# Scores of two head pairs in one visit: six half-filled PSUM banks become six nearly full ones

## The chip, the cores and the metric

The kernel runs on one core of one Trainium2 chip. The metric is the time of one execution on the device in microseconds (us), the median of several runs. One execution is also taken by the hardware profiler; its span, from the first to the last instruction, is a little shorter than the time of that same execution, and all stage times below are counted from the span's start.

## The reference

```python
def _attn_ref(q, k, v):                     # q, k, v: (8, 8, 576, 64) float32
    scores = scale * np.matmul(q, k.transpose(0, 1, 3, 2))
    rel = pos[:, None] - pos[None, :]
    mask_local = (rel >= 0) & (rel < 32)
    mask_strided = (rel >= 0) & (pos[None, :] % 32 == pos[:, None] % 32)
    # heads 0..3 take mask_local, heads 4..7 mask_strided; then softmax
    return np.matmul(attn, v)
def _moe_ref(x, w_in, w_out, alpha):        # x: (4608, 512), d_ff 2048
    h = x @ w_in
    g = np.maximum(h, 0.0) + alpha * np.minimum(h, 0.0)
    return g @ w_out
```

Attention with a different sparse mask on each half of the heads feeds a two-layer network with a PReLU between the layers. The attention output of all heads of a token is one row of x.

## The kernel before

**Attention.** The 8 batches have 8 heads each, and the kernel works on pairs of heads, 32 in all: pair g belongs to batch g//4, pairs with g%4 of 0 and 1 are local, those with 2 and 3 strided. Two neighbouring pairs of one kind are a unit u = g//2. The masks leave small dense blocks: a local head has 6 blocks of 96 queries, a strided head 8 blocks of 72. For a block, TensorE multiplies 128 keys (72 used for a strided head) by the queries over 64 rows, the head dimension. The two heads of a pair lie on partitions 0 to 63 and 64 to 127, so that their products, each half the height of the array, alternate between the halves. `score_both` (L427) makes the scores of one pair: the first group of blocks goes into `sp`, a tile of two PSUM banks, one for each head, the second into two banks `sph` of the pool `ps`. ScalarE takes exponentials into an SBUF tile `et` (L464 for `sp`, L474 twice for `sph`), and GpSimd multiplies by the 0/1 mask (L468, L470, L477). The two exponentials on `sph` are put on a list `defer`, from which each later step of attention takes one (L660); in the second half of a chunk the first of them is done at once. `pv_piece` (L486), here written P(g,a), multiplies the weights of group a of pair g by V into a `ps` bank `pv`, and VectorE evicts it with a reciprocal (L521) and a multiply (L523). Strided pairs have three such groups and local pairs two. The result is transposed into `xT`, on TensorE (`x_piece`) or by DMA (`x_dma`, with `x_copy` on ScalarE for a strided pair).

**The network.** Tokens are worked in 9 chunks of 512, n = 0 to 8. From n = 1 a chunk is a loop of 30 slots (L1025). Slots 0 to 15 (L1 here) each make one tile of the first layer: four products of 512 columns into a bank `hb` (L678), a Relu of the negative on ScalarE into `neg` (L697), and on VectorE the PReLU into `gT` (L700, deferred by the list `late` until the end of the next step). Slots 16 to 29 (L2 here) are the second layer in seven products of quarters, two slots each, with eight products of 256 columns in a slot (L811). Its operands `gsum` are sums of quarters of `gT`, made mostly on VectorE (L760), in part on GpSimd at slots 5, 9 and 13. It accumulates in three banks named A, B and C; C is used by the sixth product only (slots 26 and 27; in n = 1 slots 18 and 19).

**Order.** All work is issued in the order in which the program writes it, on each engine (`keep`). Attention from batch 2 on is cut into 97 pieces (L577 to L645), and after each slot a pace `acc` (L1039) decides how many pieces to issue. For pair g the pieces are S (the scores of pair g), P(g-1,0), perhaps a transpose of queries, X(g-2), P(g-1,1), perhaps a transpose of keys, and P(g-1,2). Some pieces carry extra work: `cast_v` on GpSimd in the first two pieces that are not S, `x_dma`, `load_d`, `load_v` or `transpose_d` after the last P, `transpose_l` or `x_copy` after the first piece. DMAs are issued from GpSimd (all that convert float32 to float16) and from SyncE.

**PSUM.** There are eight banks: `sp` has two, the pool `ps` three in rotation, and three are `hb0` to `hb2`, which `hbank` gives out to the first layer in turn and which A, B and C name in the second.

Of the kernel before, what the change touches and what calls it, by code (L numbers as in the profile page):

```python
# [9 lines left out]
F32 = mybir.dt.float32  # L10
F16 = mybir.dt.float16
ALU = mybir.AluOpType
AF = mybir.ActivationFunctionType
# [19 lines left out]
def kernel(  # L33
# [42 lines left out]
    mfirst, mother, mstr = mmul[:, 0:288], mmul[:, 96:192], mmul[0:72, 288:360]  # L76
# [22 lines left out]
    kTs = [cpool.tile([128, 2, (768, 672)[i]], F16, name=f"kT{i}") for i in range(2)]  # L99
    vls = [cpool.tile([128, 24, 65], F16, name=f"vl{i}") for i in range(2)]  # L100
    vss = [cpool.tile([128, 4, 8, 65], F16, name=f"vs{i}") for i in range(2)]
    ets = [cpool.tile([128, 800], F16, name=f"et{i}") for i in range(NE)]
    x16s = cpool.tile([80, 1024], F16)
    qks = {nm: cpool.tile([80, 4, 512], F16, name=f"{nm}sd") for nm in "qk"}

# [4 lines left out]
    def load_qk(b, strided, nm):  # L110

        h0 = 4 if strided else 0
        src = q if nm == "q" else k
        if strided and b:
            t16 = hpool.tile([128, 2, 512], F16, tag=f"{nm}s", bufs=2, name=f"{nm}s")
            cast16[(b, True, nm)] = t16
        else:
            t16 = hpool.tile([128, 2, 512], F32, tag=f"{nm}l", bufs=2, name=f"{nm}l")  # L120
            loaded[(b, strided, nm)] = t16
        base = src[b, h0 : h0 + 1, 0:1, :]
        eng = nc.sync if (b > 2 and not strided) or (b == 0 and strided) else nc.gpsimd
        if b == 0 and strided and nm == "q":
            eng = nc.scalar
        keep(eng.dma_start(t16, bass.AP(
            tensor=base.tensor, offset=base.offset,
            ap=[[8 * D, 64], [2 * S * D, 2], [S * D, 2], [1, 8 * D]])))
# [30 lines left out]
            keep(nc.sync.dma_start_transpose(o, qks[nm].rearrange("p h c -> p (h c)")))  # L159

    def cast_s(b, nm, eng):
        t16 = hpool.tile([128, 2, 512], F16, tag=f"{nm}s", bufs=2, name=f"{nm}s")
# [73 lines left out]
    ectr = {"i": 0}  # L236
# [3 lines left out]
    def make_pair(g):  # L240
        P = Pair()
        P.g, P.b, P.hp = g, g // 4, g % 4
        P.strided = P.hp >= 2
        P.pr = P.hp % 2
        P.n, P.w = (8, 72) if P.strided else (6, 96)
        u = g // 2
        P.dx = P.b >= DX and P.strided
        P.lx = P.b >= LX and not P.strided
        P.xd = P.b >= DX and P.hp < (2 if P.b == DX else 3)
        if P.dx or P.lx:  # L250
            P.qT, P.kT = (z[u % 2].rearrange("r e c -> r (e c)") for z in (qTs, kTs))
# [4 lines left out]
        if P.lx:  # L256
            P.sgroups = ([0, 1, 2, 3], [4, 5])
        P.et = {}
        P.x16 = None
        return P  # L260
# [162 lines left out]
    defer, defer_et = [], {}  # L423
    late = []
    second = {"on": False}

    def score_both(P):  # L427

        w, r = P.w, 72 if P.strided else 128
        for i in range(2):  # L430
            et = ets[ectr["i"] % NE]
            ectr["i"] += 1
            if i:
                sps = [pspool.tile([128, 512], F32, tag="ps", name="sph") for _ in range(2)]
            else:
                sp = pbpool.tile([128, 2, 512], F32, tag="sp", name="sp")
                sps = [sp[:, y] for y in range(2)]
            grp = P.sgroups[i]
            n = w * len(grp)
            for x, t in enumerate(grp):  # L440
                if P.dx:
                    q0 = k0 = 80 * (4 * (2 * P.pr + t % 2) + t // 2)
                elif P.lx:
                    j = 3 * (2 * P.pr + t % 2) + t // 2
                    q0, k0 = 96 * j, 128 * j
                else:
                    q0, k0 = w * t, 32 + 72 * t if P.strided else 96 * t
                for y in range(2):
                    hf = slice(64 * y, 64 * y + 64)
                    keep(nc.tensor.matmul(  # L450
                        sps[y][:, w * x : w * x + w], P.kT[hf, k0 : k0 + 128],
                        P.qT[hf, q0 : q0 + w], start=(x == 0), stop=(x == len(grp) - 1),
                        skip_group_check=True))
                    P.et[(2 * (t // 2) + y, t % 2) if P.dx or P.lx else (t, y)] = (et, n * y + w * x)
            ev = et[0:r, 0 : 2 * n]
            if not P.strided and i == 0 and not P.lx:
                mv = ev.rearrange("r (y c) -> r y c", y=2)
                m = mfirst.unsqueeze(1).to_broadcast([r, 2, n])
            else:
                z = 2 * w if P.lx and i == 0 else 0  # L460
                mv = ev[:, z:].rearrange("r (c f) -> r c f", f=w)
                m = (mstr if P.strided else mother).unsqueeze(1).to_broadcast([r, (2 * n - z) // w, w])
            if i == 0:
                keep(nc.scalar.activation(  # L464
                    ev.rearrange("r (y c) -> r y c", y=2), sp[0:r, :, 0:n], AF.Exp, scale=SCALE))
                if P.lx:
                    fv = ev[:, 0 : 2 * w].rearrange("r (c f) -> r c f", f=w)
                    keep(nc.gpsimd.tensor_tensor(  # L468
                        fv, fv, mfirst[:, 0:96].unsqueeze(1).to_broadcast([r, 2, w]), op=ALU.mult))
                keep(nc.gpsimd.tensor_tensor(mv, mv, m, op=ALU.mult))  # L470
                continue

            def ex(y):
                keep(nc.scalar.activation(  # L474
                    ev[:, n * y : n * y + n], sps[y][0:r, 0:n], AF.Exp, scale=SCALE))
                if y:
                    keep(nc.gpsimd.tensor_tensor(mv, mv, m, op=ALU.mult))  # L477

            defer_et["et"] = et
            if second["on"]:  # L480
                ex(0)
                defer.append(lambda: ex(1))
            else:
                defer.extend([lambda: ex(0), lambda: ex(1)])

    def pv_piece(P, a):  # L486
        run_masks(P)
        while defer and any(P.et[z][0] is defer_et["et"] for z in P.et):
            defer.pop(0)()
        if P.x16 is None:  # L490
            if P.xd and P.strided:
                P.x16 = x16s
# [25 lines left out]
        w = P.w  # L518
# [52 lines left out]
    def Pv(g, i):  # L571
        return lambda: pv_piece(pairs[g], i)
# [4 lines left out]
    for g in range(7, npair + 2):  # L577
# [75 lines left out]
    def attn_step(end):  # L653
        run_masks()
        if pos["i"] < end:
            pieces[pos["i"]][1]()
            pos["i"] += 1
        while late:
            late.pop(0)()
        if defer:  # L660
            defer.pop(0)()


    gTs = {}
# [94 lines left out]
        }[which]  # L759
        keep(eng.tensor_tensor(o[:, k0:k1], x[:, k0:k1], y[:, k0:k1], op=op))  # L760

    lay, held = {}, {}

    def store(n, i, j, osb, mts=(0, 1)):

# [310 lines left out]
```

## Time and profile before

| | us |
|---|---|
| median of 3 runs | 299.58 (299.42 to 299.84) |
| the profiled execution | 300.0 |
| its span | 298.1 |
| chunk n=1, L1 and L2 | about 59 to 75, 75 to 91.7 |
| chunk n=3, L1 and L2 | about 122.8 to 138.1, 138.1 to 153.0 |
| score visits of the pairs 8 to 31 (L450) | 24, from 61.6 to 226.9 |

The page gives, for each engine, how long it was busy and in which of 40 slices. A line of the timeline gives start, length, engine, line, operation, tiles (out<-in), shape and count of like instructions merged into one row; a bracket at its end is the time in which the engine idled before it and what it waited for. Rows of TensorE overlap, since matmuls are pipelined: a product's row is longer than the time in which the next can start.

### The profile page before, as it was taken

Reading aid. Unit: us, or ns where it says so; the run is one execution under the profiler, and the core shown is the slowest. Engines: PE = TensorE matmul, PEld = TensorE weight load, DVE = VectorE, ACT = ScalarE, POOL = GpSimd, SP = SyncE. Lnnn points to the kernel's source line nnn. Section 1 sums busy time; section 2 is a strip of 40 time slices with the busy share of each in tenths; the row PEclk is TensorE's granted clock in tenths of the full one; section 3 lists DMA queues with packets and bytes.
Section 4 is the critical chain, followed back from the end, with each engine's and each line's share of the span. In section 5 each row is a group of like instructions: output and inputs, shape, how many; then the busy total and the mean of one; then the engine's idle time right before and its main releaser. Section 6 shows DMA issues by size and latency. Waiting matters only on the chain.

```text
span 298.1 us, 7107 instructions
## 1 busy us (share of the span) xinstructions
PE 289.9 (97%) x2808; PEld 193.6 (65%) x2808; DVE 227.8 (76%) x427; ACT 173.5 (58%) x325; POOL 168.5 (57%) x182
## 2 busy tenths in 40 slices
PE   7899998999999999999999999999999999999995
PEld 3664445644886478646898887468746864784584
DVE  5788868979975988488848894889488858946872
ACT  3566556888557773776377636763676257406620
POOL 8952289359757996777777778665555003101300
PEclk9999999999999999999999999999999999999999
DMA  7999999995998969999999999993811140022004
GB/s 219 204 202 207 205 238 266 170 175 178 177 154 186 111 100 127 173 192 160 132 209 177 138 141 182 184 144 54 201 22 21 24 141 0 2 71 73 0 2 141
DMA packets 102273, 41.01 MB, mean 138 GB/s; under 512 B 80720, under 2 KB 99424, under 8 KB 102240
## 3 DMA queue, kind: packets, MB, share of 16 engines
q0 software_dynamic: 56336, 19.25, 61.1%
q1 hardware_dynamic: 45632, 20.78, 35.3%
q10 hardware_dynamic: 272, 0.52, 0.6%
q8 instruction: 22, 0.36, 0.6%
q14 instruction: 11, 0.09, 0.1%
HBM read 38.60 MB, written 9.44 MB: 161 GB/s over the span
## 4 chain that ended last, share of the span: by engine, by line
PE 80%; DMA 11%; POOL 4%; issue 2%; DVE 2%; ACT 1%; POOLq 0%
PE hb L678 36%; PE hb L811 32%; DMA ks<-in_k_dram 6%; PE pv L512 4%; DMA win<-in_moe_w_in_dram 3%; PE sp L450 2%; DMA ql<-in_q_dram 2%; PE hb L715 2%; PE opl L811 1%; PE xp L533 1%; PE tp L280 1%; DVE gT L700 1%; PE sph L450 1%; POOL ql L217 1%; POOL vl L205 0%
## 5 line engine op out<-in xcount | busy, mean ns | idle before, releaser
L678 PE MATMUL hb<-xT,win 128*128 128x512 f16 (+1 forms) x616 | 127.2, 357 | 0.0
L700 DVE SCALAR_TENSOR_TENSOR gT<-neg,oma,hb 128x512 f16<-128x512 f32 x138 | 100.7, 744 | 33.0 <-ACT neg L697 26.3
L697 ACT ACTIVATE neg<-hb 128x512 f32<-128x512 f32 x138 | 82.1, 597 | 32.7 <-PE hb L678 31.5
L678 PEld LDWEIGHTS <-win 128*128 128x128 f16 x640 | 60.0, 98 | 53.8
L760 POOL TENSOR_TENSOR gsum<-gT 128x512 f16<-128x512 f16 x23 | 26.5, 1152 | 68.9 <-DVE gT L700 68.9
L811 PEld LDWEIGHTS <-gsum 128*128 128x128 f16 x512 | 47.3, 98 | 6.0 <-DVE gsum L760 0.5
L811 PEld LDWEIGHTS <-gT 128*128 128x128 f16 x384 | 35.9, 98 | 6.0 <-issue 0.5
L470 POOL TENSOR_TENSOR et<-et,mmul 128x576 f16<-128x576 f16 (+1 forms) x24 | 30.6, 1274 | 14.6 <-issue 7.8
L823 ACT COPY o<-hb 128x512 f32<-128x512 f32 (+1 forms) x32 | 18.1, 569 | 32.5 <-PE hb L811 32.5
L523 DVE TENSOR_TENSOR x<-pv,rc 96x384 f16<-96x384 f32 (+2 forms) x65 | 34.5, 531 | 2.2
L811 PE MATMUL hb<-wout,gT 128*128 128x256 f16 x248 | 30.8, 273 | 0.1
L811 PE MATMUL hb<-wout,gsum 128*128 128x256 f16 x248 | 30.5, 272 | 0.0
L811 PE MATMUL hb<-wsum,gsum 128*128 128x256 f16 x248 | 30.3, 273 | 0.0
L477 POOL TENSOR_TENSOR et<-et,mmul 72x576 f16<-72x576 f16 (+2 forms) x24 | 29.3, 1220 | 0.4 <-ACT et L474 0.4
L826 DVE TENSOR_TENSOR o<-hb,o 128x512 f32<-128x512 f32 (+1 forms) x24 | 16.3, 681 | 17.0 <-PE hb L811 12.5
L464 ACT ACTIVATE et<-sp 72x576 f16<-72x576 f32 (+2 forms) x24 | 16.4, 685 | 20.6 <-PE sph L450 17.2
L512 PEld LDWEIGHTS <-et 72*128 72x128 f16 (+1 forms) x416 | 21.9, 98 | 8.0 <-issue 1.3
L474 ACT ACTIVATE et<-sph 72x288 f16<-72x288 f32 (+2 forms) x48 | 17.8, 388 | 0.0
L521 DVE RECIPROCAL rc<-pv 72x6 f32<-72x6 f32 (+2 forms) x80 | 14.5, 181 | 2.9 <-PE pv L512 2.4
L715 PE MATMUL hb<-wout,gT 128*128 128x512 f16 x64 | 15.6, 379 | 0.2 <-ACT osb L720 0.2
L811 PE MATMUL hb<-wsum,gT 128*128 128x256 f16 x120 | 15.3, 273 | 0.0
L760 DVE TENSOR_TENSOR gsum<-gT 128x512 f16<-128x512 f16 (+2 forms) x17 | 14.7, 865 | 0.2
(117 smaller groups left out, 318.0 us busy)
## 6 DMA issues: line engine op xcount, KB each, us to landing
out_dram<-o SPq DMA_DIRECT2D x31, 256.0 KB, 3.1
stv<-in_v_dram POOLq DMA_DIRECT2D x8, 288.0 KB, 8.4
vl<-in_v_dram POOLq DMA_DIRECT2D x6, 384.0 KB, 9.3
wout<-in_moe_w_out_dram POOLq DMA_DIRECT2D x4, 512.0 KB, 16.9
qsd<-in_q_dram POOLq DMA_DIRECT2D x6, 288.0 KB, 7.6
ksd<-in_k_dram POOLq DMA_DIRECT2D x6, 288.0 KB, 7.1
kl<-in_k_dram SPq DMA_DIRECT2D x3, 512.0 KB, 5.1
ql<-in_q_dram POOLq DMA_DIRECT2D x3, 512.0 KB, 6.4
```

Source lines behind the costliest of these rows:

```text
L470: keep(nc.gpsimd.tensor_tensor(mv, mv, m, op=ALU.mult))
L474: keep(nc.scalar.activation(ev[:, n * y : n * y + n], sps[y][0:r, 0:n], AF.Exp, scale=SCALE))
L477: keep(nc.gpsimd.tensor_tensor(mv, mv, m, op=ALU.mult))
L512: keep(nc.tensor.matmul(pv[:, 65 * x : 65 * x + 65], et[0:r, c : c + 128], v16[0:r, 2 * P.pr + hh, t, :] if P.strided else v16[:, 6 * (2 * ...
L523: keep(nc.vector.tensor_tensor(P.x16[0:w, c0 : c0 + 64 * nb].rearrange("r (c e) -> r c e", e=64), pvv[:, :, 0:64], rc[0:w, 0:nb].unsqueeze ...
L678: keep(nc.tensor.matmul(hps[:, dst : dst + w], win16[:, kk, 128 * m : 128 * m + 128], xT[:, kk, src : src + w], start=(first and kk == kks ...
L697: keep(nc.scalar.activation(neg, hps, AF.Relu, scale=-1.0))
L700: keep(nc.vector.scalar_tensor_tensor(gTs[n][:, m, :], neg, oma[:, m : m + 1], hps, op0=ALU.mult, op1=ALU.add))
L715: keep(nc.tensor.matmul(ops, gTs[n][:, kf, 128 * mt : 128 * mt + 128], wout16[:, kf, :], start=(kf == 0), stop=(kf == 15)))
L760: keep(eng.tensor_tensor(o[:, k0:k1], x[:, k0:k1], y[:, k0:k1], op=op))
L811: keep(nc.tensor.matmul(dst, lhs[:, kf, 128 * mt : 128 * mt + 128], rhs[:, kf, :], start=(first and own and kf == 0), stop=(kf == 7), skip ...
L823: keep(nc.scalar.copy(o, x))
```

## The change

`score_both` is replaced by `score_unit`, which makes the scores of both pairs of a unit, A and Bp, in one piece. It takes `sp`, three banks of `ps` (c3, c1, c2) and a sixth bank c4: one from `hbank` in L1, bank C in L2. With nb = 5 blocks of a local head or 7 of a strided one, `sp` takes the first nb blocks of both heads of A, c1 and c2 those of the two heads of Bp, and c3 and c4 the last block of both pairs. A bank is filled to 480 columns (local) or 504 (strided), c3 and c4 to 192 or 144. The matmuls are the same, in the order `sp`, c3/c4, c1/c2, always alternating between the halves. There are five exponentials for a unit instead of six, in new wide tiles `evs` (e1, e2) and an `et` tile (e3); those on c3 (in L1 only), c1 and c2 go to `defer`. The masks of a unit are five multiplies on GpSimd.

In the order of pieces, S comes for even g only, after P(g-1,0) instead of before it, and an empty piece N follows it; cast_v counts N as a place. For odd g the list begins with P(g-1,0). The tiles `evs` also serve as the buffers of the strided queries and keys of batches 0 and 1, and the six memsets of the `et` tails on GpSimd (160 columns) become four of 64.

```diff
@@ tiles @@
-    ets = [cpool.tile([128, 800], F16, name=f"et{i}") for i in range(NE)]
+    ets = [cpool.tile([128, 640], F16, name=f"et{i}") for i in range(NE)]
+    evs = [[cpool.tile([128, 1088], F16, name=f"ev{i}{j}") for j in range(2)] for i in range(2)]
@@ scores @@
-    def score_both(P):
...
+    def score_unit(u):
+
+        A, Bp = pairs[2 * u], pairs[2 * u + 1]
+        w, r, nb = A.w, 72 if A.strided else 128, 7 if A.strided else 5
+        n = nb * w
+        (e1, e2), e3 = evs[u % 2], ets[u % 2]
+        sp = pbpool.tile([128, 2, 512], F32, tag="sp", name="sp")
+        c3, c1, c2 = [pspool.tile([128, 512], F32, tag="ps", name="sph") for _ in range(3)]
+        c4 = lay["Cf"] if second["on"] else hbank()
+        rest = [(A, nb), (Bp, nb)]
+        streams = [
+            [(A, s, sp[:, 0], w * s) for s in range(nb)]
+            + [(P, s, c3, w * z) for z, (P, s) in enumerate(rest)]
+            + [(Bp, s, c1, w * s) for s in range(nb)],
+            [(A, s, sp[:, 1], w * s) for s in range(nb)]
+            + [(P, s, c4, w * z) for z, (P, s) in enumerate(rest)]
+            + [(Bp, s, c2, w * s) for s in range(nb)],
+        ]
+        for x in range(2 * nb + 2):
+            for y in range(2):
+                P, s, o, c = streams[y][x]
...
+        def ex3():
+            ev = e3[0:r, 0 : 4 * w]
+            ex(ev[:, 0 : 2 * w], c3[0:r, 0 : 2 * w])
+            mask(ev.rearrange("r (c f) -> r c f", f=w),
+                 (mstr if A.strided else mother).unsqueeze(1).to_broadcast([r, 4, w]))
+
+        def ex2():
+            ex(e2[0:r, n : 2 * n], c2[0:r, 0:n])
+            masks(e2)
+
+        ex(e1[0:r, 0 : 2 * n].rearrange("r (y c) -> r y c", y=2), sp[0:r, :, 0:n])
+        ex(e3[0:r, 2 * w : 4 * w], c4[0:r, 0 : 2 * w])
+        masks(e1)
+        if second["on"]:
+            ex3()
+        else:
+            defer.append(((e3,), ex3))
+        defer.append(((e2,), lambda: ex(e2[0:r, 0:n], c1[0:r, 0:n])))
+        defer.append(((e2,), ex2))
@@ order of pieces @@
-        if okA:
-            seq.append(("S", lambda a=a: score_both(pairs[a])))
         if okP:
             seq.append(("P", Pv(p, 0)))
+        if okA and a % 2 == 0:
+            seq.append(("S", lambda a=a: score_unit(a // 2)))
+            seq.append(("N", lambda: None))
@@ start @@
         if m == 6:
-            for t in ets:
-                keep(nc.gpsimd.memset(t[:, 640:800], 0.0))
+            for t in evs[0] + evs[1]:
+                keep(nc.gpsimd.memset(t[:, 1024:1088], 0.0))
```

More of the change, by code (lines that the diff above doesn't have):

```diff
@@ L116, in load_qk @@
         if strided and b:
-            t16 = hpool.tile([128, 2, 512], F16, tag=f"{nm}s", bufs=2, name=f"{nm}s")
+            t16 = evs[b]["qk".index(nm)][:, 0:1024].rearrange("p (f c) -> p f c", f=2)
             cast16[(b, True, nm)] = t16
@@ L161, in cast_s @@
     def cast_s(b, nm, eng):
-        t16 = hpool.tile([128, 2, 512], F16, tag=f"{nm}s", bufs=2, name=f"{nm}s")
+        t16 = evs[b]["qk".index(nm)][:, 0:1024].rearrange("p (f c) -> p f c", f=2)
         if eng[0] == eng[1]:
@@ L255, in make_pair @@
         P.pgroups = ([0, 1, 2], [3, 4, 5], [6, 7]) if P.strided else P.sgroups
-        if P.lx:
-            P.sgroups = ([0, 1, 2, 3], [4, 5])
         P.et = {}
@@ L421, in score_piece @@
         keep(nc.gpsimd.tensor_tensor(ev, ev, m, op=ALU.mult))
-    defer, defer_et = [], {}
+    defer = []
     late = []
+    lay = {}
     second = {"on": False}
-    def score_both(P):
[L429 to L440, printed above, removed]
+    def score_unit(u):
[18 more added lines that the diff above has]
+                P, s, o, c = streams[y][x]
@@ L441, in score_both @@
                 if P.dx:
-                    q0 = k0 = 80 * (4 * (2 * P.pr + t % 2) + t // 2)
+                    q0 = k0 = 80 * (4 * (2 * P.pr + s % 2) + s // 2)
                 elif P.lx:
-                    j = 3 * (2 * P.pr + t % 2) + t // 2
+                    j = 3 * (2 * P.pr + s % 2) + s // 2
                     q0, k0 = 96 * j, 128 * j
                 else:
[L447 to L458, printed above, removed]
-            else:
[L460 to L484, printed above, removed]
+                    q0, k0 = w * s, 96 * s
@@ new lines, in score_unit, with mask @@
+                hf = slice(64 * y, 64 * y + 64)
+                keep(nc.tensor.matmul(
+                    o[:, c : c + w], P.kT[hf, k0 : k0 + 128], P.qT[hf, q0 : q0 + w],
+                    start=(c == 0), stop=(c == (1 if s == nb else nb - 1) * w), skip_group_check=True))
+                key = (2 * (s // 2) + y, s % 2) if P.dx or P.lx else (s, y)
+                P.et[key] = (e3, 2 * w * y + c) if s == nb else (e1 if P is A else e2, n * y + c)
+        def mask(v, m):
+            keep(nc.gpsimd.tensor_tensor(v, v, m, op=ALU.mult))
@@ new lines, in masks @@
+        def masks(e):
+            ev = e[0:r, 0 : 2 * n]
+            if A.lx:
+                fv = ev[:, 0 : 2 * w].rearrange("r (c f) -> r c f", f=w)
+                mask(fv, mfirst[:, 0:96].unsqueeze(1).to_broadcast([r, 2, w]))
+                fv = ev[:, 2 * w :].rearrange("r (c f) -> r c f", f=w)
+                mask(fv, mother.unsqueeze(1).to_broadcast([r, 2 * nb - 2, w]))
+                return
+            k = 4 if A.strided else 3
+            fv = ev.rearrange("r (y c) -> r y c", y=2)
+            if A.strided:
+                m = mstr
+                for lo, hi in ((0, k), (k, nb)):
+                    mask(fv[:, :, w * lo : w * hi].rearrange("r y (c f) -> r y c f", f=w),
+                         m.unsqueeze(1).unsqueeze(1).to_broadcast([r, 2, hi - lo, w]))
+            else:
+                mask(fv[:, :, 0 : w * k], mfirst.unsqueeze(1).to_broadcast([r, 2, w * k]))
+                mask(fv[:, :, w * k :].rearrange("r y (c f) -> r y c f", f=w),
+                     mother.unsqueeze(1).unsqueeze(1).to_broadcast([r, 2, nb - k, w]))
@@ new lines, in ex @@
+        def ex(o, i):
+            keep(nc.scalar.activation(o, i, AF.Exp, scale=SCALE))
+        def ex3():
[7 more added lines that the diff above has]
+        ex(e1[0:r, 0 : 2 * n].rearrange("r (y c) -> r y c", y=2), sp[0:r, :, 0:n])
@@ L486, in pv_piece @@
+        ex(e3[0:r, 2 * w : 4 * w], c4[0:r, 0 : 2 * w])
[6 more added lines that the diff above has]
+        defer.append(((e2,), ex2))
     def pv_piece(P, a):
         run_masks(P)
-        while defer and any(P.et[z][0] is defer_et["et"] for z in P.et):
-            defer.pop(0)()
+        used = [P.et[t, y][0] for t in P.pgroups[a] for y in range(2)]
@@ L490, in pv_piece @@
+        while any(e is z for es, _ in defer for e in es for z in used):
+            defer.pop(0)[1]()
         if P.x16 is None:
@@ L660, in attn_step @@
         if defer:
-            defer.pop(0)()
+            defer.pop(0)[1]()
     gTs = {}
@@ L760, in g_sum @@
         keep(eng.tensor_tensor(o[:, k0:k1], x[:, k0:k1], y[:, k0:k1], op=op))
-    lay, held = {}, {}
+    held = {}
     def store(n, i, j, osb, mts=(0, 1)):
```

## The prediction, made before the result was known

> **What bounds the kernel now.** I read the page first (busy time, slices, chain), then the waits, then the timelines of single engines around score visits.
>
> ```profile
> PE 289.9 (97%) x2808; PEld 193.6 (65%) x2808; DVE 227.8 (76%) x427; ACT 173.5 (58%) x325; POOL 168.5 (57%) x182
> ...
> PEclk9999999999999999999999999999999999999999
> ```
>
> TensorE is the bound, at full clock, and the chain is 80% PE. The waits view (us in total, times, longest) adds a line:
>
> ```profile
> PEld L450 <- issue: 6.8, 22, 0.4
> ```
>
> So the weight loads of the score matmuls (L450) sat idle 22 times, about 0.31 us each: something happens whenever PE turns to half-height products. The timeline of PE in chunk n=3 (start, length, last column the count) shows what:
>
> ```profile
> 142.57 0.60 PE L811 MATMUL hb<-wsum,gsum 128*128 128x256 f16 x4
> 143.10 0.34 PE L450 MATMUL sp<-qT,kT 64*128 64x96 f16 x8
> 143.28 0.25 PE L450 MATMUL sph<-qT,kT 64*128 64x96 f16 x4
> 143.47 1.05 PE L811 MATMUL hb<-wsum,gsum 128*128 128x256 f16 x8
> 144.59 0.34 PE L512 MATMUL pv<-vs,et 72*128 72x65 f16 x6
> ```
>
> Eight L811 products take 0.875 us, 109 ns each. Four from 142.57 end at 143.01, but L450 starts at 143.10: 0.09 lost going in. Eight score products take 0.18 (a pair of heads per 45 ns, side by side), so the twelve end near 143.37; L811 resumes at 143.47, 0.10 lost going out. A third loss: L811 should end at 144.35, but the next pv starts at 144.59, 0.24 late. Its PSUM bank is the reason, as VectorE's timeline shows:
>
> ```profile
> 142.21 0.55 DVE L523 TENSOR_TENSOR x16s<-pv,rc 72x384 f16<-72x384 f32 x1
> 142.69 1.21 DVE L760 TENSOR_TENSOR gsum<-gT,gsum 128x2048 f16<-128x2048 f16 x1
> 143.82 0.17 DVE L521 RECIPROCAL rc<-pv 72x4 f32<-72x4 f32 x1
> 144.03 0.42 DVE L523 TENSOR_TENSOR x16s<-pv,rc 72x256 f16<-72x256 f32 x1
> 144.37 1.21 DVE L760 TENSOR_TENSOR gsum<-gT 128x2048 f16<-128x2048 f16 x1
> 145.50 0.18 DVE L521 RECIPROCAL rc<-pv 72x6 f32<-72x6 f32 x1
> 145.72 0.56 DVE L523 TENSOR_TENSOR x<-pv,rc 72x384 f16<-72x384 f32 x1
> ```
>
> VectorE runs without a gap from 138.98 to 146.28. The eviction ending at 144.45 frees the ps bank that the pv at 144.59 takes (0.14 later). GpSimd's timeline in n=1:
>
> ```profile
> 62.95 1.28 POOL L470 TENSOR_TENSOR et<-et,mmul 128x576 f16<-128x576 f16 x1 [7.85 <-issue]
> 64.18 2.01 POOL L217 COPY vs<-stv 72x1024 f16<-72x1024 f16 x2
> ...
> 82.49 0.76 POOL L197 DMA_DIRECT2D stv<-in_v_dram  x1
> 85.59 1.27 POOL L470 TENSOR_TENSOR et<-et,mmul 128x576 f16<-128x576 f16 x1 [2.35 <-ACT et L464]
> 86.83 1.26 POOL L477 TENSOR_TENSOR et<-et,mmul 128x576 f16<-128x576 f16 x1
> 91.58 2.02 POOL L217 COPY vs<-stv 72x1024 f16<-72x1024 f16 x2 [3.49 <-DMA stv<-in_v_dram]
> ```
>
> Here the cast of batch 3's V waits for its load until 91.58, with the score masks safely ahead of it.
>
> [...]
>
> **The change, part by part** (L1 = slots 0 to 15, L2 = slots 16 to 29 of a chunk; a slot of L2 is 0.875 us, a tile of L1 0.864 us, a pv piece 0.19).
>
> 1. *Visits.* 24 become 12, with the same 336 matmuls. A visit costs 0.46 us (143.01 to 143.47), of which 12 or 16 matmuls stream for 0.26; what goes is one entry and one exit, 0.09+0.10 plus 0.01 on the first product after: 0.208. 12 x 0.208 = **-2.5**.
>
> 2. *The pv wait* above recurs in n=3, 4, 5 (at 144.6, 174.9, 205.1), 0.24 each. With two ps tiles fewer between, that pv finds its bank free: **-0.7**.
>
> 3. *GpSimd memsets* (L986): six of 128x160, 1.12 us on the chain at 40.8, become four of 128x64: 0.30 by columns, 0.75 by count. PE waits 0.7 for GpSimd soon after. I take **-0.4**, ends 0 and -0.8.
>
> 4. *Third ps bank in L2.* The visit now wants all three ps banks, and the piece in front of it is P(g-1,0), whose pv holds one; before, S came first and took two older banks. n=3: L2's slot 4 ends at 143.01, the pv adds 0.19, slot 5 0.875, so the visit starts at 144.16, and c2 (eighth of twelve pairs, 7 x 0.043 later) is wanted at 144.47. VectorE evicts that pv at 145.50 to 146.28 because its queue, in program order, is full. The pv of P(4n+5,1) also moves three slots later in L1, so that VectorE enters L2 0.14 later. 146.28+0.14+0.14 = 146.56: PE waits 2.09 us with all of lin2 behind it. n=4 and 5 repeat the pattern 30 us apart (evictions end 176.58, 206.74): 3 x 2.07 = **+6.2**. n=2: eviction could end 115.90, plus 0.28, wanted 115.41: **+0.7**. n=1: **+0.2**. c4 is lin2's bank C there, unused until slot 26: nothing.
>
> 5. *c4 in L1* takes one of lin1's three banks, so the reuse distance falls. Relu 0.60 and PReLU 0.745 with their latencies free a tile's bank 1.63 us after its last product (0.20+0.60+0.03+0.745+0.05); three tiles give 1.73. The tile after the visit takes the bank of the tile before last: free at 1.63-0.86 = 0.77, wanted at 0.72, plus VectorE's arrears from the P before (0.14 after two tiles, 0.31 after one): 0.05 in the first visit, 0.2 in four, 0.35 in two: 1.55. ScalarE's three exponentials in a row (estimate 0.92+0.2+0.2, from 576 wide in 0.54 start to start and 0.9 ns a column) hold the next Relu by about 0.1, nearly inside the slack. **+1.6**, ends 0.5 and 2.6. Exponential columns are the same; only bunching costs.
>
> 6. *GpSimd in n=1.* First visit at 61.5: two masks of it from 63.3, the e3 mask to 66.3, V casts 2.0 to 68.3, gsum 1.1 to 69.4, and only then e2's first mask, to 70.6. P(9,0) moves ahead of S, two slots earlier: 61.5+0.77+8 tiles+2 pieces = 69.5. **+1.1**, ends 0 and 1.5. Second: cast_v(3,0) now goes ahead of unit 6's masks and waits for DMA till 91.58 (GpSimd reaches that load at about 82.5 as before). Cast 0.98, first mask 1.27: 93.85. P(12,0), at 90.39 before, comes at about 91.5. **+2.3**; ends 0 (load lands early) and 4.8 (loads of vl, qsd, ksd leave some 3 us later and crowd it).
>
> 7. *Moved and hidden.* load_d of c+1 goes three slots later: 133.2 becomes about 136.3, landed by 144.7 (median 7.6), and SP's transposes ran at 145.78 behind x_dma anyway; without that cover SP is late, PE is not, since the data is used a chunk later. x_copy moves from S's slot to P(g,0)'s: ScalarE is idle there now that the exponentials come earlier. load_v and load_l keep their slots. Elsewhere the first cast_v (1.0) precedes e1's masks, five slots before their use. One more mask per unit costs GpSimd about 0.2, hidden likewise.
>
> Sum: -2.5-0.7-0.4+6.2+0.7+0.2+1.6+1.1+2.3 = **+8.5** on the profiled execution's 300.0 us (span 298.1 and 1.9 around it), that is 308.5. The median of the runs is 299.6, 0.4 lower: **308.1**.
>
> **Rivals.** (A) All waits as above: 308.1, 305.5 to 311 by the ends; 0.58. (B) PSUM waits only: n=1's masks come in time, -3.4: 304.7, down to 301.5 with VectorE's arrears one piece smaller (3 x 0.7) and L1 at its low end; for it, GpSimd idles 2.35 and 1.58 in n=1; against it, strict order at the cast; 0.22. (C) The other side: banks are free when wanted. Place: c2 in L2, and c4's neighbours. It decides at 144.4: if the preceding pv is evicted by then (VectorE ahead of its gsum steps by 1.9 us), 8.7 goes: 299.4, and 296.0 if the pv also relieves n=1. For it: that pv is issued 1.5 us earlier than before. Against: VectorE has no gap to take it in. 0.13. (D) Heavier: late masks also hold P(2u,0) elsewhere, or V lands late: 312 to 314; 0.07. That the change doesn't merge visits I exclude[...].
>
> **Numbers.** 0.2% (0.6 us) is about what a measurement can tell. C splits into faster 0.08 and same 0.05; the rest, 0.87, is slower. Leaving out C and D (0.2) gives 301.5 to 311.
>
> **What would show it.** Right: 12 visits of about 0.73 us plus a hole before c2 of some 2 us in n=3, 4, 5, ended by the eviction of the preceding pv; no 0.24 hole at the next pv; a PE wait on masks at P(12,0) near 91 to 94. Wrong: c2 following c1 without a hole, or the V cast of n=1 landing before 89.

## The result, and the profile after

The changed kernel takes **325.21 us** (median of four runs, 324.29 to 326.36) against 299.71 us (299.42 to 300.34) for the kernel before on the same chip: a ratio of **1.085** (95% interval 1.081 to 1.089). The forecast was 308.1, with a range up to 311. The direction and most of the places were right; the size was not. The span of the profiled execution grew from 298.1 to 324.6 us, by 26.5.

The first thing to look at in the page of the changed kernel is TensorE's busy share beside the clock row:

```profile
PE 299.8 (92%) x2808; PEld 199.0 (61%) x2808; DVE 233.9 (72%) x427; ACT 172.7 (53%) x313; POOL 172.2 (53%) x186
...
PEclk9999999999996999999799987999799999999999
```

TensorE does the same 2808 products, but it is busy 9.9 us longer, and it idles 24.8 us of the span instead of 8.2. The clock row, which was all nines, has dips in the slices near 100, 155 to 165, 195 to 200 and 230 us. The forecast noted the full clock of before and had no term for a change in it. The waits view (us in total, times, longest) says who was waited for:

```profile
PEld L456 <- DVE x L546: 6.5, 5, 2.0
...
PE sph L456 <- DVE x L546: 5.8, 4, 1.9
...
PE pv L535 <- POOL ev L463: 5.1, 3, 4.2
...
PEld L835 <- DVE gsum L784: 3.5, 7, 1.1
...
PEld L456 <- issue: 3.4, 11, 0.4
```

The last row answers to the 22 idle weight loads of before (6.8 us): half of them are gone, as forecast. The others are new. In TensorE's timeline of chunk n=3 the first pair of them shows as the hole that was forecast in front of c2, with another in front of c1, which was not:

```profile
155.11 0.39 PE L456 MATMUL sp<-qT,kT 64*128 64x96 f16 x10
...
156.31 0.21 PE L456 MATMUL sph<-qT,kT 64*128 64x96 f16 x1 [0.73 <-DVE x16s L546]
158.43 0.58 PE L456 MATMUL sph<-qT,kT 64*128 64x96 f16 x9 [1.91 <-DVE x L546]
158.94 4.01 PE L835 MATMUL hb<-wout,gsum 128*128 128x256 f16 x24
```

By the starts of single products, c1 comes 0.89 us late and c2 another 2.08. Then look at the last row: 24 products of 256 columns end 4.01 us after their start; at the 109 ns of before they need 24 x 0.109 = 2.6 us and the tail of the last. Eleven of the single starts stand 213 ns apart: the clock is halved there, in the records from 158.05 to 161.47. VectorE's timeline of the same stretch shows why the eviction that c2 waits for (ending at 158.36) is so late:

```profile
150.31 0.83 DVE L784 TENSOR_TENSOR gsum<-gT 128x512 f16<-128x512 f16 x1
151.07 2.12 DVE L784 TENSOR_TENSOR gsum<-gsum,gT 128x1024 f16<-128x1024 f16 x2
...
156.17 1.51 DVE L784 TENSOR_TENSOR gsum<-gT 128x2048 f16<-128x2048 f16 x1
...
157.81 0.55 DVE L546 TENSOR_TENSOR x<-pv,rc 72x384 f16<-72x384 f32 x1
```

Before, the same sums took 0.42, 1.28 for two, 1.21 and 1.21 (the last two stand in the prediction):

```profile
139.76 0.42 DVE L760 TENSOR_TENSOR gsum<-gT 128x512 f16<-128x512 f16 x1
140.10 1.28 DVE L760 TENSOR_TENSOR gsum<-gsum,gT 128x1024 f16<-128x1024 f16 x2
```

Here three of the five are longer, by 0.41, 0.83 (one of the pair) and 0.30 us. Chunk n=1 holds the largest single wait, 4.33 us by product starts and 0.69 more for the next mask. Slow products follow again: eight that took 0.875 us now take 1.69, from 98.94 to 100.63, where the next row begins:

```profile
97.49 0.40 PE L535 MATMUL pv<-vl,ev 128*128 128x65 f16 x4 [4.17 <-POOL ev L463]
...
98.94 1.90 PE L835 MATMUL hb<-wsum,gT 128*128 128x256 f16 x8
```

GpSimd's timeline gives the cause, the V cast that stands ahead of the masks and waits for its load, issued at 83.17:

```profile
78.52 3.19 POOL L463 TENSOR_TENSOR ev<-ev,mmul 72x576 f16<-72x576 f16 x2
...
95.17 1.03 POOL L218 COPY vs<-stv 72x1024 f16<-72x1024 f16 x1 [11.29 <-DMA stv<-in_v_dram]
96.17 2.13 POOL L463 TENSOR_TENSOR ev<-ev,mmul 128x576 f16<-128x576 f16 x2
```

The first of these rows matters too: two masks run from 78.52 to 81.7, just when VectorE makes the first sums of that second half. One 1024-column sum takes its usual 0.69, the next two 3.17 together:

```profile
78.48 0.69 DVE L784 TENSOR_TENSOR gsum<-gT 128x1024 f16<-128x1024 f16 x1
79.09 3.17 DVE L784 TENSOR_TENSOR gsum<-gsum,gT 128x1024 f16<-128x1024 f16 x2
```

By stages, from the start of each first layer and second layer in both traces, the growth is: start to the end of n=1's L1 +0.68; n=1 L2 +8.24; n=2 L1 +1.51 (its first 2.8 us at half clock, to 103.44); n=3, 4 and 5 L2 +4.46, +5.82 and +5.22; everything else 0.26 or less each. The L1 halves of n=3 to 5 changed by -0.02 to -0.08.

So the theory after the result: the waits are those of the forecast, some larger; two things that it lacks do the rest. A long wait of TensorE is paid a second time, at half clock. And VectorE's sums slow down when GpSimd works at the same time, which makes both the sums and the evictions behind them late. The rivals: the long products are a trait of the records or of contention on TensorE; the long sums have another cause.

### The profile page after: what moved, and what is told of

Read it like the earlier page. It is cut to its first block, busy times and chain, and to the rows that moved or that the text cites. A ratio compares the mean times of both kernels' runs of the same rounds, so it can differ in the third digit from the quotient of the medians.

```text
span 324.6 us, 7079 instructions
## 1 busy us (share of the span) xinstructions
PE 299.8 (92%) x2808; PEld 199.0 (61%) x2808; DVE 233.9 (72%) x427; ACT 172.7 (53%) x313; POOL 172.2 (53%) x186
## 4 chain that ended last, share of the span: by engine, by line
PE 55%; DVE 16%; DMA 11%; POOL 8%; issue 7%; ACT 2%; POOLq 0%; ACTq 0%; DVEq 0%
PE hb L702 27%; PE hb L835 21%; DVE gsum L784 6%; DMA ev<-in_k_dram 5%; DVE gT L724 5%; DMA win<-in_moe_w_in_dram 3%; POOL ev L463 3%; DMA kl<-in_k_dram 2%; DVE x L546 2%; PE pv L535 2%; DVE x16s L546 2%; PE hb L739 2%; ACT neg L721 1%; PE opl L835 1%; POOL vl L206 1%
## 5 line engine op out<-in xcount | busy, mean ns | idle before, releaser
L702 PEld LDWEIGHTS <-win 128*128 128x128 f16 x640 | 61.5, 98 | 57.2 <-issue 3.9
L463 POOL TENSOR_TENSOR ev<-ev,mmul 72x576 f16<-72x576 f16 (+5 forms) x48 | 55.8, 1173 | 30.2 <-ACT ev L486 29.2
L784 POOL TENSOR_TENSOR gsum<-gT 128x512 f16<-128x512 f16 x23 | 26.5, 1152 | 77.4 <-DVE gT L724 53.0
L835 PEld LDWEIGHTS <-gsum 128*128 128x128 f16 x512 | 50.0, 103 | 11.6 <-DVE gsum L784 3.5
L835 PE MATMUL hb<-wout,gsum 128*128 128x256 f16 x248 | 35.2, 302 | 0.0
L535 PEld LDWEIGHTS <-ev 72*128 72x128 f16 (+1 forms) x288 | 17.1, 99 | 11.6 <-POOL ev L463 5.9
L218 POOL COPY vs<-stv 72x1024 f16<-72x1024 f16 x12 | 15.6, 1306 | 11.3 <-DMA stv<-in_v_dram 11.3
L214 ACT COPY xT<-xp 128x576 f16<-128x576 f16 x11 | 7.0, 641 | 26.3 <-PE xp L556 26.2
L486 ACT ACTIVATE ev<-sph 128x480 f16<-128x480 f32 (+1 forms) x24 | 13.7, 595 | 5.4 <-PE sph L456 5.4
L835 PE MATMUL hb<-wsum,gT 128*128 128x256 f16 x120 | 16.1, 282 | 0.0
L784 DVE TENSOR_TENSOR gsum<-gT 128x512 f16<-128x512 f16 (+2 forms) x17 | 15.7, 926 | 0.2
```

What stands on the lines that cost most here:

```text
L218: keep(nc.gpsimd.tensor_copy(o, i))
L463: keep(nc.gpsimd.tensor_tensor(v, v, m, op=ALU.mult))
L535: keep(nc.tensor.matmul(pv[:, 65 * x : 65 * x + 65], et[0:r, c : c + 128], v16[0:r, 2 * P.pr + hh, t, :] if P.strided else v16[:, 6 * (2 * ...
L702: keep(nc.tensor.matmul(hps[:, dst : dst + w], win16[:, kk, 128 * m : 128 * m + 128], xT[:, kk, src : src + w], start=(first and kk == kks ...
L835: keep(nc.tensor.matmul(dst, lhs[:, kf, 128 * mt : 128 * mt + 128], rhs[:, kf, :], start=(first and own and kf == 0), stop=(kf == 7), skip ...
```

## The experiments

None of the kernels here leaves out any of the reference's computation; the ones that add work say what. A time without a range is that of a single execution.

**The V cast behind the visit.** One edit to the changed kernel: extra work goes only to pieces after S.

```diff
-        nslots = [i for i, z in enumerate(seq) if z[0][0] != "S"] or list(range(len(seq)))
+        sat = max([i for i, z in enumerate(seq) if z[0] == "S"], default=-1)
+        nslots = [i for i in range(len(seq)) if i > sat] or [len(seq) - 1]
```

> Only the place of the V casts changes: they are issued after S, not before it. If the cast at the head of GpSimd's queue is what held the masks in n=1, the 4.33 us hole before P(12,0) goes, and with it the slow products behind it (about 2.1 us): 325.2 - 6.5 = 318.7, with the holes of n=3, 4, 5 as they were. If the masks are late for another reason (GpSimd simply overloaded), the hole stays above 2 us and the time above 322.

Measured: 314.06. The wait at P(12,0) is gone and n=1 L2 grows by 2.21 instead of 8.24, n=2 L1 by 0.13 instead of 1.51. So the place of the casts on GpSimd's queue alone was worth 11 us, more than expected, since the second halves of n=3 to 5 improved too: their growth is 3.57, 3.56 and 3.58. TensorE's timeline in n=3:

```profile
149.72 0.38 PE L456 MATMUL sph<-qT,kT 64*128 64x96 f16 x9 [1.61 <-DVE x L546]
150.03 4.46 PE L836 MATMUL hb<-wout,gsum 128*128 128x256 f16 x24
```

The two waits are 0.52 and 1.78 by product starts, 2.3 together: close to the 2.07 of the forecast. The pair of 1024-column sums took 1.28 here, and the 0.24 wait at the next pv, which was still there in the changed kernel, is gone as forecast. The next row begins at 154.33, and the 24 products before it need 2.6 us at full clock: 1.7 is lost to the clock. 2.3 + 1.7 - 0.2 (one visit less) - 0.24 (that pv wait) = 3.6, which is the growth of the half.

**The order of S and P.** Two kernels, both with the cast behind S; the first puts S ahead of P(g-1,0), the second puts the empty piece first and P last.

```diff
-        if okP:
-            seq.append(("P", Pv(p, 0)))
         if okA and a % 2 == 0:
             seq.append(("S", lambda a=a: score_unit(a // 2)))
+        if okP:
+            seq.append(("P", Pv(p, 0)))
+        if okA and a % 2 == 0:
             seq.append(("N", lambda: None))
```

> S goes back in front of P(g-1,0), the casts behind S. If c1 and c2 wait for the eviction of the pv pieces just before them, the visit in L2 now waits for P(.,2) of one slot earlier only: a hole of about 1 us in place of 3.0 in n=3, 4, 5, no slow products after it, and no hole in n=1: 325.2 - 6.5 - 3 x 4 = about 307. If VectorE's backlog or ScalarE's longer exponentials hold PE whatever the order, the time stays at 315 to 319.

> The empty piece comes first, then S, then P(g-1,0): one more slot between the last pv and the visit. If the bank wait is a matter of distance, the hole in L2 falls under 0.5 us: 301 to 303, near the kernel before. If not, 307 or more as with S first.

Measured: 305.65 for S, P, N, as expected, and 309.54 for N, S, P, not as expected. In the second halves of n=3 to 5 the theory holds in both: the wait for the third bank is 1.14 each with S, P, N (the halves grow by 0.72 to 0.75) and 0.35 to 0.38 with N, S, P, where these halves are as long as before (-0.02 to -0.06). The granted clock is full throughout in both (mean 1.00). The products of c1 and c2 that waited, in n=3 of the first kernel and then of the second (the bracket counts only the idle time; the starts before are 145.61 and 150.48):

```profile
146.79 0.38 PE L456 MATMUL sph<-qT,kT 64*128 64x96 f16 x9 [0.98 <-DVE x16s L546]
```

```profile
150.90 0.38 PE L456 MATMUL sph<-qT,kT 64*128 64x96 f16 x9 [0.22 <-DVE x16s L546]
```

What is new is outside these halves. With N, S, P the waits move to n=1 (masks in L1, +2.23; L2 +2.87, of which a pv waits 1.43 for an exponential, and sums and one PReLU account for 1.9) and to the start of L1 in n=4 and 5 (+1.21 and +1.68: the first tiles wait for `xT`, copied late by ScalarE behind its DMA). With S, P, N they go to L1, +0.28 to +1.23 in each chunk.

**Holes of five lengths.** The kernel before, with TensorE made to wait for 1 to 5 memsets of GpSimd (0.95 us each) in chunks 7 and 8, where the attention is over: a spare product that reads the tile that the memsets fill.

```diff
+    def hole(k):
+        dm = pspool.tile([128, 512], F32, tag="ps", name="dm")
+        for z in range(2):
+            keep(nc.tensor.matmul(dm[:, 0:128], hd[:, 0:128], hd[:, 128:256], start=True, stop=True))
+            if z == 0:
+                for _ in range(k):
+                    keep(nc.gpsimd.memset(hd, 0.25))
...
+    HOLES = {(7, 2): 1, (7, 12): 2, (7, 22): 3, (8, 2): 4, (8, 12): 5}
```

> The kernel before, with five artificial waits of PE in chunks 7 and 8, where attention is over: PE waits for one to five memsets of 1024 columns on GpSimd[...]. If a wait costs its own length only, 299.7 + 14 = about 314. If a long wait also slows the clock afterwards, the products behind the longer ones take twice their time for some microseconds, behind the shorter ones not: 317 to 320, and the length from which it happens is read from the trace. The extra products write a spare bank that nothing reads.

Measured: 326.44, 26 above the kernel before. The holes are 1.23, 2.30, 3.31, 4.32 and 5.33 us by product starts, 16.5 in all; the other 9 to 10 us are lost afterwards. After 1.23 us no product is slow. The second hole in TensorE's timeline:

```profile
257.46 0.23 PE L670 MATMUL dm<-qT 128*128 128x128 f16 x1 [2.14 <-POOL qT L673]
257.52 4.44 PE L687 MATMUL hb<-xT,win 128*128 128x512 f16 x12
```

The twelve 512-column products took 4.44 us; a row of twelve elsewhere takes 2.75. By single starts, 8 of them stand 427 ns apart instead of 216 after the hole of 2.30 (1.6 us lost, beginning 0.55 after work resumed), 16 of 256 columns 213 instead of 109 after that of 3.31 (1.7 lost), 14 of 512 after that of 4.32 (2.9), and 16 after that of 5.33 (2.9). The length-only rival, 314, is out. The windows view gives the granted clock of a stretch (third number from the end, behind start and end, length, and the busy times of TensorE, its weight loads, VectorE, ScalarE and GpSimd). Here are the second hole and, in the changed kernel, n=3:

```profile
254.48:257.90 3.42, 1.28 (x8) 0.54 (x7) 1.97 (x3) 1.15 (x2) 2.40 (x3) 1.00 0.03 5
257.90:261.31 3.41, 3.41 (x10) 1.21 (x8) 0.75 (x1) 1.10 (x2) 0.62 (x1) 0.50 0.00 0
```

```profile
154.64:158.05 3.41, 1.15 (x20) 0.65 (x18) 3.34 (x6) 1.91 (x4) 3.25 (x4) 1.00 1.34 149
158.05:161.47 3.42, 3.04 (x21) 2.17 (x22) 0.32 (x1) 1.03 (x2) 3.42 (x5) 0.50 2.27 154
```

The moments at which the clock halves lie on a grid. In the ladder they are 257.90, 271.55, 285.20 and 302.27, in the changed kernel 96.61, 158.05, 192.19 and 229.73: their distances are 4, 4 and 5 and 18, 10 and 11 times 3.413 us, and the half clock lasts one or two such steps. In the step before each of the eight, and before the three in n=3 to 5 of the first experiment, TensorE was idle for 1.7 us or more of the 3.41 by its busy time; in no other step of the changed kernel, from 50 to 290 us, was it idle for more than 1.4. So the idle time within one step seems to count, in one wait or in several, rather than the length of a wait. This is read from the traces; no run moves a wait along the grid. It is not the whole account either: in the first experiment (mean clock 0.976 over 312.2 us, some 15 us at half) the clock is also at half from 17.15 to 20.56, after a step in which TensorE was busy with small products for 3.28 us.

**The waits filled with work.** This tests the clock in the changed kernel itself: every wait is left as it is, but TensorE is given spare products to do in the four longest.

```diff
+    def fill(o, k):
+        for _ in range(k):
+            keep(nc.tensor.matmul(o, win16[:, 0, 0:128], win16[:, 0, 0:512], start=True, stop=True))
...
+        if u in (10, 12, 14):
+            fill(c4, 11)
...
+        if (P.g, a) == (12, 0):
+            fill(pv, 19)
```

> The changed kernel with idle time of TensorE filled and nothing else: nineteen spare products of 128x512 (4.1 us, into the bank that the following products overwrite, output unchanged) ahead of P(12,0) in chunk 1, where TensorE waits 4.33 for masks, and eleven (2.4 us, into the visit's own bank, before it is used) ahead of the visit in the second half of chunks 3, 4 and 5, where it waits 3.0, 3.0 and 2.7 in all for the third ps bank. What TensorE waits for stays as late as it was. Clock theory (a long wait is followed by some us at half clock, 7.7 us in all): no product at twice its duration, granted clock 1.0, second half of chunk 1 shorter by about 2.1 and those of chunks 3 to 5 by 1 to 2.7 each; run 317 to 320. Rival theory (the long products are a matter of the records, or of what TensorE contends with, and the time is all waiting): the run stays at 325, or gets longer by what the spare products delay.

Measured: 317.7 (316.43 to 318.27; 1.0544 times the kernel before, 1.047 to 1.062). With 52 products more, the kernel is faster. The clock row, and n=3 in TensorE's timeline:

```profile
PEclk9999999999999999999999999999999999999999
```

```profile
152.43 2.54 PE L429 MATMUL hb<-win 128*128 128x512 f16 x11
...
155.85 0.38 PE L462 MATMUL sph<-qT,kT 64*128 64x96 f16 x9 [0.44 <-DVE x L554]
156.17 2.79 PE L843 MATMUL hb<-wout,gsum 128*128 128x256 f16 x24
```

The 24 products behind the visit take 2.79 us instead of 4.01, and no product is at twice its duration. In both kernels c2 resumes 9.82 us after the start of this half, so the wait itself was not shortened. The span is 316.2 against 324.6: the half clock cost **8.4 us** of the changed kernel's 26.5.

**Sums beside GpSimd.** The kernel before with GpSimd work that nobody needs beside VectorE's sums, once with masks and once with memsets; in a second kernel with DMA issues and with copies.

```diff
...
+                if (n, i) == (7, 15):
+                    for _ in range(6):
+                        keep(nc.gpsimd.tensor_tensor(
+                            hv, hv, mother.unsqueeze(1).to_broadcast([128, 6, 96]), op=ALU.mult))
+                if (n, i) == (8, 15):
+                    for _ in range(10):
+                        keep(nc.gpsimd.memset(hd, 0.25))
```

> The kernel before, with extra GpSimd work beside VectorE's G sums where the attention is over: six in-place mask products of 128x576 (two SBUF inputs) put at the end of chunk 7's first half, ten memsets of 128x576 (no input) at the end of chunk 8's. Nothing on TensorE waits for them; the output is unchanged. Contention theory (VectorE's sums with two SBUF inputs slow down while GpSimd reads SBUF): the 683 ns and 1215 ns sums of chunk 7 become 1.3 to 1.8 us each while the mask products run, those of chunk 8 stay at 683 and 1215 ns; total up by 1 to 3 us, all in chunk 7. Rival theory (the sums in the changed kernel were long for another reason, such as a DMA issue or a wait inside the record): all sums stay within 3% of 683 and 1215 ns, and the total stays at that of the kernel before.

Measured: 303.54. VectorE's timeline, chunk 7 beside masks and chunk 8 beside memsets:

```profile
258.82 3.44 DVE L762 TENSOR_TENSOR gsum<-gsum,gT 128x1024 f16<-128x1024 f16 x2
...
264.40 2.29 DVE L762 TENSOR_TENSOR gsum<-gT 128x2048 f16<-128x2048 f16 x1
...
287.76 1.28 DVE L762 TENSOR_TENSOR gsum<-gsum,gT 128x1024 f16<-128x1024 f16 x2
```

Beside masks a 1024-column sum takes 1.76 us instead of 0.68 and a 2048-column one 2.2 to 2.3 instead of 1.22; beside memsets nothing changes. The masks suffer too: 1.28 us alone, 1.60 to 2.14 beside the sums. TensorE waited for these sums four times (0.29 to 1.07 idle, 3.1 in all by product starts), which is most of the 3.6 by which the span grew, a little above the 1 to 3 expected. GpSimd's timeline shows the six masks as one row, which ends at 265.61:

```profile
255.99 9.62 POOL L1037 TENSOR_TENSOR qT<-qT,mmul 128x576 f16<-128x576 f16 x6
```

The sum beside the last mask ends at 266.69, 1.08 us after it; by single instructions each 1024-column sum ends 0.55 us after the mask beside it, and each of the last three masks 1.13 after the sum before it. By these times the two engines take turns, each held up by the instruction of the other. The same 0.55 stands behind both slow sums of n=1 in the changed kernel, and 1.08 between the V cast of n=3 and the last sum (156.17, ending at 157.68):

```profile
154.92 1.68 POOL L218 COPY vs<-stv 72x1024 f16<-72x1024 f16 x1
```

> The kernel before, with extra GpSimd work again beside VectorE's G sums of chunks 7 and 8, of the two kinds that stood beside a slow sum in the changed kernel and weren't tried yet: six DMA issues (a reload of the strided Q and K of batch 7, whose data nobody uses again) at the end of chunk 7's first half, six copies of 128x1024 (one SBUF input) at the end of chunk 8's. The output is unchanged. Theory[...]: chunk 7's sums stay at 683 and 1215 ns, chunk 8's become 1.3 to 2.3 us each while the copies run; total up by 1 to 3 us. Rival theory (a DMA issue on GpSimd does it too, as the 1517 ns sums of chunks 3 and 4 suggest, which had only issues beside them): chunk 7's sums are long as well.

```diff
...
+                if (n, i) == (7, 15):
+                    for _ in range(3):
+                        load_d(7)
+                if (n, i) == (8, 15):
+                    for _ in range(6):
+                        keep(nc.gpsimd.tensor_copy(hd, kd))
```

Measured: 303.09, against 301.31 for the kernel before beside it (one execution each). VectorE's timeline in chunk 8:

```profile
285.61 2.96 DVE L762 TENSOR_TENSOR gsum<-gsum,gT 128x1024 f16<-128x1024 f16 x2
...
290.47 1.21 DVE L762 TENSOR_TENSOR gsum<-gT 128x2048 f16<-128x2048 f16 x1
```

Copies with one SBUF input do it as well: 1.52 us each for the 1024-column pair, and the last sum, after the copies, is back at 1.21. Chunk 7's sums kept their durations, but this half is weak: GpSimd waited for its DMA queue, and only one issue (261.83 to 262.53) fell beside a sum, which took its usual 1.22.

**The order by halves.** An attempt to take the best of each order: P, S, N in the first half, N, S, P in the second from batch 5 on, S, P, N in the second before that, casts behind S.

```diff
...
+        if not (okA and not a & 1):
+            seq += pvp
+        elif a // 2 & 1:
+            seq += pvp + [scr, pad]
+        elif a < 20:
+            seq += [scr] + pvp + [pad]
+        else:
+            seq += [pad] + [scr] + pvp
```

> The changed kernel with three edits: V casts only behind the visit in their group (as in the run with only that edit), in the second half of a chunk from batch 5 on the order padding, visit, P(g-1,0), in the second half before that visit, P(g-1,0), padding; in the first half the order of the change is kept (P, visit, padding). Theory (the loss of chunks 3 to 5 is the wait for the third ps bank and the slow clock after it, the losses of the other two orders are their own first halves): second halves of chunks 3 to 5 within 0.3 of the kernel before with a hole of 0.3 to 0.6 at the visit, first halves within 0.2 but for 0.7 in chunk 1, full clock; run 300.9, 300.0 to 302.0. Rival theory (VectorE comes out of such a first half with too much queued, whatever the order in the second): holes of 1 us or more in chunks 3 to 5, run 303 to 305.

> As the run with the order by halves, with one more empty slot ahead of the visit in the second half from batch 5 on (padding, padding, visit, P). Theory (what remains of the hole is VectorE's lateness, about 0.4 us, and one slot more gives it 0.9 us): the holes at the visit of chunks 3 to 5 are gone (below 0.1 each), run 1.0 below that run, about 299.9. Rival theory (the wait moves to the next taker of a bank, the P behind the visit): same time as that run within 0.3.

Measured: 307.31 (1.0265 times before, 1.0246 to 1.0284) and, with one more empty piece, 305.38. Neither theory has the first number. The holes are 0.65 to 0.69 instead of 0.3 to 0.6, and the halves of n=3 to 5 grow by 0.25 to 0.29; 2.27 comes from n=1 L2, where masks run beside the sums as in the changed kernel, and 0.46 and 0.92 from L1 of n=4 and 5. With the second padding the holes are gone, but the P behind the visit then waits 0.45 for an exponential in each of these halves, which still grow by 0.16 to 0.19. So the wait moves to the next piece, near what the rival said, though not for a bank. The time of the rival did not come: the span is 1.0 shorter (303.6 against 304.6), as the theory said, the largest part of it in L1 of n=5.

**The masks of n=1 held back.** The order by halves, with no deferred exponential or mask issued in slots 14 to 17 of n=1.

```diff
-        if defer:
+        if defer and not hold["on"]:
             defer.pop(0)[1]()
...
+            hold["on"] = n == 1 and 14 <= i < 18
```

> The kernel with the order by halves (307.3) with one edit: in slots 14 to 17 of chunk 1 no deferred exponential or mask is issued, so that GpSimd's masks of the second pair come after VectorE's three G sums and ScalarE's exponentials after the last tiles' Relu. Contention theory (those sums took 0.69 and 1.6 each because of the masks): the sums take 0.68 each, TensorE's waits of 1.12 and 0.96 at the start of that second half go, chunk 1 is shorter by 1.3 to 2.1, run 305.2 to 306. Rival theory (the sums are long because of TensorE's or the DMAs' traffic at that place): sums and waits stay, run 307.3 or later.

Measured: 305.65. VectorE's first sums of n=1 with the masks out of the way:

```profile
79.09 1.29 DVE L790 TENSOR_TENSOR gsum<-gsum,gT 128x1024 f16<-128x1024 f16 x2
```

The pair of 1024-column sums takes 1.29 instead of 3.17, TensorE's waits of 0.30 and 0.96 for the sums are gone, the one of 1.12 for the PReLU is 0.65, and n=1 L2 grows by 0.41 instead of 2.27. Of this gain of 1.9 the span keeps 0.7 (303.9 against 304.6): the time up to the second half of n=1 and L1 of n=4 are about 0.5 longer each.

None of these versions beats the kernel before; the best are 5 to 6 us slower. Halves that show no growth exist (n=3 to 5 L2 with N, S, P; L1 with P, S, N), but the two orders could not be had together without a wait elsewhere.

## Why the prediction was wrong

By its own terms, the forecast sum is +8.5; the terms measured are these (waits by product starts, against the kernel before):

| term | forecast | measured |
|---|---|---|
| 1 visits | -2.5 | -2.4 |
| 2 pv wait in n=3 to 5 | -0.7 | 0 |
| 3 memsets | -0.4 | 0 |
| 4 third bank: n=3, 4, 5; n=2; n=1 | +6.2; +0.7; +0.2 | +8.6; +0.3; +0.5 |
| 5 c4 in L1 | +1.6 | +0.8 |
| 6 P(9,0); P(12,0) | +1.1; +2.3 | +0.6; +5.0 |
| not in it: sums (2.6) and a PReLU in n=1 (0.9) that TensorE waits for | 0 | +3.5 |
| not in it: half clock | 0 | +8.4 |
| sum | +8.5 | +25.3 |

The span grew by 26.5; some 1.2 is spread over waits too small to count here.

- **Right: term 1.** An entry costs 0.096 and an exit 0.095, with 0.48 to 0.50 of matmuls in between; with the 0.01 on the product after, twelve of these are gone: 12 x 0.2.
- **Right in mechanism: terms 4 and 6.** TensorE waits in front of c2 for the eviction of the preceding pv, with the second layer behind it, 1.8 to 2.1 us each, and 0.9 before in front of c1, for an earlier eviction; with the sums at their old duration but for one (first experiment) the two are 2.3 together, near the 2.07 forecast. The rest, some 0.7, comes with the longer sums. At P(12,0) the masks come behind the cast: the load landed 12 us after its issue instead of 9, which is the upper end that the forecast gave (4.8) and did not take.
- **Failed: "with two ps tiles fewer between, that pv finds its bank free"** (term 2). In the changed kernel it waits 0.25 as before. The reason is VectorE's lateness, not the count of tiles: in the first experiment, where the pair of 1024-column sums kept its duration in n=3, the wait is gone.
- **Failed: term 3.** The four memsets are shorter, but the mask product behind them (`mmul`, L1011) went from 1.47 to 2.26 us; both chains end at 43.5, 1.3 us after a copy on VectorE (41.43 to 42.19 before, 41.56 to 42.26 after). What made it longer, this copy or the sum of weights ahead of it, was not tested.
- **Half: terms 5 and P(9,0).** The exits from L1's visits cost 0.05 to 0.28 beyond the 0.095, not 0.2 to 0.35. P(9,0) waited 0.6: an empty slot also takes one exponential from `defer`, so that the e2 mask came before GpSimd's sum, not behind it.
- **Failed: what a wait costs.** The sum prices every wait at its length and puts the clock at nothing. The long waits cost TensorE 1.4 to 2.9 us more each at half clock, 8.4 us in all: half of the error, and alone more than the range allowed. The ladder of holes shows it after a single wait of 2.30 us, the first experiment after 0.52 and 1.78 close together, and the run with the waits filled (mean clock 1.00) has no such loss.
- **Failed: durations of before.** An engine's instruction was priced at its duration of before, though the change moved GpSimd's masks beside VectorE's sums: 2.6 us of waits for sums that the forecast does not have (and 0.9 for a PReLU that waited for ScalarE), and part of the 2.4 by which term 4 in n=3 to 5 was too small. The added work beside the sums shows the same: a 1024-column sum went from 0.68 to 1.76 us beside masks and to 1.52 beside copies, and did not change beside memsets.

What stays open: the 1024-column sum of 1.52 us in n=3 and n=4 (the longest delay there, 0.83) has exactly the duration that the copies gave in the last contention run, but the records show only DMA issues of GpSimd beside it, and at the same place in the first experiment, with the same issues, it took 0.68. Issues alone were hardly tested. Nor was it followed up why N, S, P delays the copies into `xT` in n=4 and 5.

## What to carry to other kernels

A new wait of TensorE of up to 1.2 us cost its length here; one of 2.3 us, or two that added up to it within a step of 3.4 us, cost 1.4 to 3 us more. Cutting a wait below that, or giving TensorE spare work in it (8.4 us here, for four waits), was then worth more than its length suggests. When a change moves work on one queue, look at what it then runs beside: VectorE's sums of two SBUF tiles took 1.5 to 1.8 us instead of 0.68 beside GpSimd's masks and copies here, and are better kept apart from them where either is waited for. And a merged step wants all its banks at once; the saving of its fewer entries (0.2 us each here) is small against one late eviction.

## What the hardware showed that was not expected

- A wait of 2.30 us was enough for half clock, 1.23 us was not (nor 1.14 in the order S, P, N); waits of 0.52 and 1.78 us with one product pair between were enough too, and whether the second alone is isn't shown. The eight halvings read here lie on a grid of 3.413 us and last one or two steps; in the ladder they come 0.44 and 0.27 us after the end of the holes of 2.30 and 3.31, and 0.89 and 0.82 before the end of those of 4.32 and 5.33. So 3.4 us of work ran slow after the first two and 6 us after the others.
- Spare products made a kernel 7.5 us faster (325.2 to 317.7; the kernel before stood at 299.7 and 300.4 beside them; 8.4 by the spans).
- The contention goes both ways: beside masks the sum took 1.76 us instead of 0.68 and the mask 1.60 instead of 1.28; beside copies the sum took 1.52 and the copy 1.38 instead of 1.04. The longer times fit two engines that take turns: a 2048-column sum ended 1.08 us after the mask or the copy beside it, in the changed kernel too.
